# Attention values in one run per set, and a new order of ScalarE and VectorE work in the second pass of a sparse-attention and feed-forward kernel

## The chip, the cores and the metric

One core of a Trainium2 chip. The metric is the device time in microseconds of one execution, as the median of several runs; lower is better. A profile of one execution gives the times of single instructions.

## The reference

Block-sparse attention over 4 batches, 8 heads, 768 positions and a head size of 64, followed by a feed-forward layer with softplus between its two matrices. A position's block of 32 sees the neighbouring blocks, the first, the last, and three sampled ones; the rows of the first and last block see everything.

```python
def _attn_ref(q, k, v, sampled_blocks):
    scores = scale * np.matmul(q, k.transpose(0, 1, 3, 2))
    mask = np.abs(blk_i - blk_j) <= window
    mask = mask | (blk_i == 0) | (blk_j == 0) | (blk_i == n_blocks - 1) | (blk_j == n_blocks - 1)
    ...
            mask[qb * block:(qb + 1) * block, kb * block:(kb + 1) * block] = True
    scores = np.where(mask, scores, -1000000000.0)
    ...
    return np.matmul(attn, v)

def _moe_ref(x, w_in, w_out):          # x is 3072 x 512, d_ff 2048
    h = x @ w_in
    g = np.maximum(h, 0.0) + np.log1p(np.exp(-np.abs(h)))
    return g @ w_out
```

## The kernel before

**Attention.** The work is cut into 28 sets: per batch five sparse sets of four query blocks, a whole set (the first and last block, which see all keys) and a sparse set of the last two query blocks, folded onto the partitions. Each set has two units (`NA` is 2), a unit being four heads. A unit goes through `scores` (TensorE, PE below; then VectorE, DVE below, masks them, L831), `exponents` (ScalarE, ACT below, L881), `transposes` (PE L894, copied to SBUF tiles `pt`, of which there are four) and `values` (PE L937, L924 or L951: weights of 32 or 64 columns, so that several outputs lie side by side on the array). Both units of a set write one PSUM tile, which `normalise` reads after the second; `turn` transposes the result (L980) and `x_high` and `x_low` (L995, L999) split it into two parts for matmuls in two terms. The values of a set are partly gathered by indirect DMAs, which GpSimd (POOL below) issues (L764), into one of two buffers; `load_values` for the set after next is queued when a set's second unit has its values.

`pieces(n)` cuts a unit's work into three pieces, each with parts of several units: `scores` of unit n+2, then `exponents` of n+2, `turn` of the set before and `values` of n, then `transposes` of n+1.

**Feed-forward.** Its steps `j` run through `seq`: the first pass takes 6 of the 16 slices of d_ff for 8 tiles of 384 tokens (48 steps) and shares its time with attention, piece by piece by due times (`due`); the second pass takes the other 10 slices for 6 tiles of 512 tokens (60 steps). A step spreads over the following ones: `hidden(j)` is the first matrix (L268 to L270) with Abs and Exp on ACT (L272, L277; in combined steps also the relu, L275); `rounding(j)` the copy plus one on ACT (L283) and two operations on DVE (L285, and L287 or L289); then `logarithm` (ACT L294), `softplus` (DVE L316 or L322), `high` (ACT L347 or L343, the part rounded for the matmul), `low` (DVE L359 or L354, the rest) and, three steps later, `project`, the second matrix.

Forty steps of the second pass (tiles 1 to 4) are combined: two slices by two halves of the tokens are multiplied with seven products in place of eight. `combine` (POOL L337) forms the sums of the inputs, `project_item` (L437 to L439) adds into seven PSUM sums in seven banks, so that `h` has one bank in these steps. After the last slice of a tile, `store_item` puts the sums together for each half: two copies on ACT (L455, L457), four additions on DVE that read PSUM (L456, L458 to L460), then six additions on POOL (L464) and two stores, which `add_later` issues four at a time behind the `combine` of the next steps.

**What sets the order.** The order on SP, which issues most DMAs, is that of the program throughout. In the second pass the order on ACT, DVE and POOL is that of the program too. In the first pass these engines, and PE always, are ordered by a planner that follows the program's order with its own costs for each instruction.

```python
def first_half(j):
    for stage, n in ((high, j - 2), (logarithm, j - 1), (hidden, j)):
def second_half(j):
    for stage, n in (
        (softplus, j - 1), (combine, j - 1), (add_later, j - 1), (low, j - 2), (rounding, j), (project, j - LEAD)
    ):
```

Of the kernel before, what the change touches and what calls it, by code (L numbers as in the profile page):

```python
# [15 lines left out]
ALU = mybir.AluOpType  # L16
# [11 lines left out]
EARLY = 6  # L28
# [29 lines left out]
def sparse_attention_ffn(  # L58
# [22 lines left out]
    nc = tc.nc  # L81
# [4 lines left out]
    NA = NP // 2  # L86
# [8 lines left out]
    NTB = NT // TB  # L95
# [254 lines left out]
    def low(n):  # L350
# [5 lines left out]
        if not combined(n):  # L356
# [2 lines left out]
            nc.vector.tensor_tensor(out=gl, in0=l, in1=G[n].bitcast(F32), op=ALU.subtract)  # L359
            G[n] = (G[n], gl)  # L360

    def first_half(j):
        for stage, n in ((high, j - 2), (logarithm, j - 1), (hidden, j)):
            if 0 <= n < len(seq):
                stage(n)

# [35 lines left out]
    acc = {}  # L402
# [7 lines left out]
    def sums_of(half, m):  # L410
        if m == 4:
            return acc[2][:, half * SUB : (half + 1) * SUB]
        bank, at = ((0, 0), (1, 0), (1, 1), (2, 0), None, (0, 1), (2, 1))[m]
        return acc[half][bank][:, at * SUB : (at + 1) * SUB]
# [25 lines left out]
        if last:  # L440
            store_item(2 * t + half)

    later_sums = []

    def store_item(u):
        half = u % 2
        na, nb = 2 * u, 2 * u + 1
        ya, yb = Y.pop(na), Y.pop(nb)
        m1, u2, u3, m5 = [
            gp.tile([P, SUB], F32, tag=tag, name=f"{tag}_{u}_{x}") for tag in ("e", "u") for x in range(2)  # L450
        ] if half == 0 else [
            gp.tile([P, SUB], F32, tag=tag, name=f"{tag}_{u}_{x}") for tag in ("gh", "gl") for x in range(2)
        ]
        left, right = slice(0, SUB), slice(SUB, DM)
        nc.scalar.copy(out=m1, in_=sums_of(half, 0))  # L455
        nc.vector.tensor_tensor(out=yb, in0=acc[half][1], in1=yb, op=ALU.add)  # L456
        nc.scalar.copy(out=m5, in_=sums_of(half, 4))  # L457
        nc.vector.tensor_tensor(out=u2, in0=sums_of(half, 5), in1=m1, op=ALU.add)  # L458
        nc.vector.tensor_tensor(out=ya[:, left], in0=ya[:, left], in1=sums_of(half, 3), op=ALU.subtract)
        nc.vector.tensor_tensor(out=u3, in0=sums_of(half, 6), in1=u2, op=ALU.add)  # L460
        for out_, more in (
            (u2, m5), (m5, u3), (yb[:, left], m1), (yb[:, right], u2), (ya[:, left], u3), (ya[:, right], m5),
        ):
            later_sums.append((lambda o=out_, x=more: nc.gpsimd.tensor_tensor(out=o, in0=o, in1=x, op=ALU.add)))  # L464
        later_sums.append((lambda: put(nb, yb)))
        later_sums.append((lambda: put(na, ya)))

    def add_later(n):
        for _ in range(4):
            if later_sums:  # L470
                later_sums.pop(0)()
# [27 lines left out]
    def put(n, y):  # L499
        b, g = order[n]  # L500
        lo = b * S + (4 * g + 1) * BLOCK
        rows = P if g < NG - 1 else P - BLOCK
        nc.sync.dma_start(out=out[lo : lo + rows], in_=y[0:rows])
        if rows < P:
            nc.sync.dma_start(out=out[b * S : b * S + BLOCK], in_=y[rows:P])
# [45 lines left out]
    for rows in (slice(0, NR * BLOCK), slice(NR * BLOCK, P)):  # L551
# [4 lines left out]
        out=vbuf[0][:, 0, 0, :], out_offset=None, in_=v,  # L556
# [69 lines left out]
    def load_kT(b, n, engine=nc.sync, parts=4):  # L626
        load_part(b, n * NB // parts, (n + 1) * NB // parts, engine)
# [30 lines left out]
    def gathered(work, m):  # L658
        while work and work[0][0] <= m:
            work.pop(0)[1]()  # L660
# [54 lines left out]
    sets = []  # L715
# [62 lines left out]
    units = [(m, a) for m in range(len(sets)) for a in range(NA)]  # L778
# [127 lines left out]
    def values(n):  # L906
        m, a = units[n]
        b, g, whole = sets[m]
        pt = state[n]["pt"]
        gathered(value_work, m)  # L910
        vd = vg[sets[m]]
        if a == 0:
            xps[m] = ps_x.tile([P, DM], F32, tag="x", name=f"x{n}")
        xq = xps[m]

        if not whole and g == NG - 1:
            for r in range(2):
                at = (2 * a + r) * D
                for c in range(2):
                    for j in range(2):  # L920
                        h = 2 * (2 * a + j) + r
                        for i in range(2):
                            rows = slice((2 * j + i) * BLOCK, (2 * j + i + 1) * BLOCK)
                            nc.tensor.matmul(  # L924
                                xq[rows, at : at + D],
                                pt[r, c][:, rows],
                                vd[:, c, i, h * D : (h + 1) * D],
                                start=(c == 0), stop=(c == 1),
                            )
        elif not whole:  # L930
            for j in range(2):
                for r in range(2):
                    h = 2 * (2 * a + j) + r
                    for c in range(2):
                        for i in range(NI):
                            rows = slice(i * BLOCK, (i + 1) * BLOCK)
                            nc.tensor.matmul(  # L937
                                xq[rows, h * D : (h + 1) * D],
                                pt[r, 2 * j + c][:, rows],
                                vd[:, c, i, h * D : (h + 1) * D],  # L940
                                start=(c == 0), stop=(c == 1),
                            )
        else:
            rows_v = vd.rearrange("p c i f -> p (c i) f")
            for r in range(2):
                at = (2 * a + r) * D
                for c in range(NCH):
                    for o in range(2):
                        rows = slice(64 * o, 64 * o + 64)
                        h = 2 * (2 * a + o) + r  # L950
                        nc.tensor.matmul(  # L951
                            xq[rows, at : at + D],
                            pt[r, c][:, rows],
                            rows_v[:, c, h * D : (h + 1) * D],
                            start=(c == 0), stop=(c == NCH - 1),
                        )
# [47 lines left out]
    def pieces(n):  # L1004

        ended = [units[i][0] if 0 <= i < len(units) and units[i][1] == NA - 1 else None for i in range(n - 2, n + 1)]

        scored = None
        if n + 2 < len(units) and units[n + 2][1] == NA - 1 and not sets[units[n + 2][0]][2]:
            scored = place[sets[units[n + 2][0]][:2]]  # L1010

        def score_piece():
            if ended[0] is not None:
                x_low(ended[0])
            s = n + 2
            if s < len(units):
                scores(s)
                if scored is not None:
                    load_keys(scored + 2)
                m, a = units[s]  # L1020
                b, g, whole = sets[m]
                if whole and a == NA - 1 and b + 1 < B:

                    gathered(key_work, place[b, g])
                    for n_ in range(4):
                        load_kT(b + 1, n_)
                    load_keys()

        def value_piece():
            if n + 2 < len(units):  # L1030
                exponents(n + 2)
            if ended[1] is not None:
                turn(ended[1])
            if n < len(units):
                values(n)
                if ended[2] is not None:
                    load_values(ended[2] + 2)
            if scored is not None:
                load_queries(scored + 2)

        def transpose_piece():
            if ended[1] is not None:
                x_high(ended[1])
            if ended[2] is not None:
                normalise(ended[2])
            if n + 1 < len(units):
                transposes(n + 1)

        return score_piece, value_piece, transpose_piece


# [52 lines left out]
        gather()  # L1104
        convert()

    SECOND = NTB * EARLY
    owed = 0.0

    def convert():  # L1110
# [38 lines left out]
    for j in range(len(seq) + LEAD):  # L1149
        if j >= SECOND:  # L1150
            phase, t, f = seq[j] if j < len(seq) else (3, 0, 0)
# [4 lines left out]
        for i in range(NPAIR):  # L1156
            at = SECOND + LEAD + 1 + i
            if j == at:
# [3 lines left out]
            if j == at + 3 + (i == NPAIR - 1):  # L1162
                split_pair(i)
        if j == SECOND - 3:
            load_x(0)
        if j == SECOND:
            ctx.enter_context(tc.manual_schedule(
# [13 lines left out]
        if done == len(attention) and ahead is None:  # L1181
# [5 lines left out]
            ahead = EARLY  # L1187
        while ahead is not None and ahead < min(NF, EARLY + 2 * (j + EARLY - SECOND + 1)):
            load_w2(ahead)
            ahead += 1  # L1190

        for _ in range(1 + j % 2):
            if j >= SECOND - 4 and parked:
                split_w2(*parked.pop(0))
# [38 lines left out]
```

## Time and profile before

| | |
|---|---|
| median of 3 runs | 805.89 us (804.74 to 806.54) |
| the profiled execution | 804.17 us, span 802.4 us |
| PE busy | 764.1 us (95%) |
| DVE, ACT, POOL busy | 591.3, 562.0, 398.1 us |
| DMA | 132.27 MB, mean 165 GB/s |

Times are microseconds from the start of the span. PE is the matmul part of TensorE, PEld its weight loads. In a row of a group of instructions stand line, engine, operation, `out<-in` with the program's tile names, shape and count, then busy time, mean ns of one, and the idle time ahead of them with what ended it. A row of waits names who waited, for whom, the total, the number and the longest. In a timeline a row has start, duration, engine, line and, in brackets, the idle time before it. Up to about 65 us only attention runs; until about 420 us attention and the first pass share the core, and the second pass starts at about 461 us.

### The profile page before, as it was taken

The page shows a single profiled execution, that of the slowest core. Times are in us where ns is not written, and L with a number is a line of the kernel's source. Part 1 is how long each engine was busy: PE and PEld are TensorE (multiplying, and loading weights), DVE is VectorE, ACT ScalarE, POOL GpSimd, SP SyncE. Part 2 cuts the span into 40 slices and gives each one's busy share as a digit, 9 for nine tenths or more (in the row PEclk, how much of TensorE's full clock was granted, in tenths as well). Part 3 has the DMA queues.
Part 4 walks back from the last instruction along what each step waited for, and adds up shares of the span by engine and source line. Part 5 has one row for each costly group of instructions (what it writes and reads, how often), then busy time and mean ns, then how long its engine had stood idle before and what let it go on. Part 6 is the DMA issues. An engine that isn't in the chain of part 4 may idle for free.

```text
span 802.4 us, 21570 instructions
## 1 busy us (share of the span) xinstructions
PE 764.1 (95%) x8188; PEld 620.0 (77%) x8188; DVE 591.3 (74%) x1292; ACT 562.0 (70%) x1235; POOL 398.1 (50%) x617
## 2 busy tenths in 40 slices
PE   8779979999999999999999999999999999999997
PEld 7546657777778777687788888888988988988786
DVE  6678898787877777785664658886687787876654
ACT  4777878876877777776766766777666757756552
POOL 6783776544565427564000006435487686595400
PEclk9899989999999999999999999999999999999999
DMA  8878897678797686956525764330303215020021
GB/s 246 251 226 278 258 255 246 186 254 285 205 282 222 217 287 190 287 146 191 181 76 188 231 232 168 105 107 1 105 27 107 79 40 171 14 67 26 27 79 52
DMA packets 61174, 132.27 MB, mean 165 GB/s; under 512 B 5712, under 2 KB 18128, under 8 KB 60048
## 3 DMA queue, kind: packets, MB, share of 16 engines
q1 hardware_dynamic: 55072, 112.41, 44.4%
q0 software_dynamic: 5712, 17.57, 7.7%
q8 instruction: 64, 1.05, 0.6%
q10 hardware_dynamic: 288, 0.93, 0.3%
q14 instruction: 38, 0.31, 0.1%
HBM read 100.47 MB, written 30.41 MB: 163 GB/s over the span
## 4 chain that ended last, share of the span: by engine, by line
PE 49%; DVE 18%; ACT 17%; POOL 6%; issue 5%; DMA 3%; another core or an unknown queue 1%; SPq 0%; ACTq 0%; DVEq 0%; POOLq 0%
PE h L268 7%; PE h L270 6%; PE h L269 6%; ACT pr L881 6%; POOL gq L337 4%; PE o L486 4%; PE o L487 4%; PE o L488 4%; DVE e L285 3%; PE t L894 3%; PE x L937 3%; PE s L825 2%; DVE gl L359 2%; PE acc L439 2%; PE acc L438 2%
## 5 line engine op out<-in xcount | busy, mean ns | idle before, releaser
L337 POOL TENSOR_TENSOR gq<-gq 128x128 f32<-128x128 f32 x160 | 112.1, 723 | 76.3 <-DVE gq L322 73.2
L285 DVE SCALAR_TENSOR_TENSOR e<-u,e 128x512 f32<-128x512 f32 (+1 forms) x108 | 84.5, 782 | 84.8 <-ACT u L283 81.7
L881 ACT ACTIVATE pr<-pr,nmax 128x256 f32<-128x256 f32 (+1 forms) x192 | 102.2, 534 | 30.9 <-DVE nmax L831 14.1
L764 POOL DMA_INDIRECT vg<-in_v_dram,ix x88 | 88.2, 1003 | 67.8 <-PE x L937 38.6
L706 POOL COPY kg<-kT 128x128 f32 x252 | 88.2, 394 | 44.5 <-PE s L825 38.3
L272 ACT ACTIVATE e<-h 128x512 f32<-128x512 f32 (+1 forms) x108 | 58.8, 544 | 71.5 <-PE h L270 71.2
L268 PE MATMUL h<-x,w 128*128 128x512 f32 x240 | 95.8, 399 | 6.4 <-ACT gh L275 4.9
L270 PE MATMUL h<-x,w 128*128 128x512 f32 x240 | 94.6, 394 | 0.0
L269 PE MATMUL h<-x,w 128*128 128x512 f32 x240 | 94.6, 394 | 0.0
L294 ACT ACTIVATE u<-u 128x512 f32<-128x512 f32 (+1 forms) x108 | 62.9, 582 | 24.2 <-DVE e L285 23.5
L193 POOL TENSOR_TENSOR wt<-wt,raw 128x512 int32<-128x512 int32 x32 | 43.5, 1360 | 68.8 <-ACT raw L170 51.8
L283 ACT ACTIVATE u<-e 128x512 f32<-128x512 f32 (+1 forms) x108 | 63.1, 584 | 17.9 <-DVE gl L359 14.3
L268 PE MATMUL h<-x,w1all 128*128 128x384 f32 x192 | 69.0, 360 | 3.4 <-DVE e L289 2.3
L831 DVE CUSTOM_DVE_ANT_1 pr<-s,mask 128x256 f32<-128x256 f32 x160 | 58.2, 418 | 16.8 <-PE s L825 8.8
L894 PE MATMUL t<-ident,pr 128*128 128x128 f32 x448 | 65.2, 286 | 4.4 <-DVE nmax L831 2.0
L343 ACT CAST w1all<-gq 128x896 fp32r<-128x896 f32 x40 | 37.7, 942 | 39.4 <-POOL gq L337 37.4
L270 PE MATMUL h<-x,w1all 128*128 128x384 f32 x192 | 65.2, 340 | 0.0
L269 PE MATMUL h<-x,w1all 128*128 128x384 f32 x192 | 65.2, 340 | 0.0
L277 ACT ACTIVATE e<-e 128x512 f32<-128x512 f32 (+1 forms) x108 | 63.1, 584 | 1.8
L486 PE MATMUL o<-w1all,gh 128*128 128x512 f32 x144 | 61.0, 424 | 0.0
L894 PEld LDWEIGHTS t<-ident,pr 128*128 128x128 f32 x448 | 50.8, 145 | 13.0 <-issue 2.7
L268 PEld LDWEIGHTS h<-x,w 128*128 128x128 f32 x240 | 45.0, 188 | 17.9 <-ACT gh L275 6.3
(141 smaller groups left out, 2051.1 us busy)
## 6 DMA issues: line engine op xcount, KB each, us to landing
vg<-in_v_dram SPq DMA_DIRECT2D x19, 768.0 KB
xD<-x SPq DMA_DIRECT2D x8, 1536.0 KB
raw<-in_w_in_dram SPq DMA_DIRECT2D x16, 512.0 KB
raw<-in_w_out_dram SPq DMA_DIRECT2D x16, 512.0 KB
qc<-in_q_dram SPq DMA_DIRECT2D x24, 256.0 KB
vg<-in_v_dram SPq DMA_DIRECT2D x12, 512.0 KB
yD<-os SPq DMA_DIRECT2D x24, 256.0 KB
x<-xD SPq DMA_DIRECT2D x4, 1536.0 KB
```

Source lines behind the costliest of these rows:

```text
L268: nc.tensor.matmul(ph, wh[:, cols], hi[:, c], start=(c == 0), stop=False)
L269: nc.tensor.matmul(ph, wh[:, cols], lo[:, c], start=False, stop=False)
L270: nc.tensor.matmul(ph, wl[:, cols], hi[:, c], start=False, stop=(c == NC - 1))
L277: nc.scalar.activation(e, e, AF.Exp, scale=-1.0)
L283: nc.scalar.activation(u, e, AF.Copy, bias=1.0)
L285: nc.vector.scalar_tensor_tensor(out=e, in0=u, scalar=-1.0, in1=e, op0=ALU.add, op1=ALU.subtract)
L337: nc.gpsimd.tensor_tensor(out=a[:, to], in0=a[:, x], in1=a[:, y], op=op)
L486: nc.tensor.matmul(po[m], gh[:, cols], wh, start=first, stop=False)
L706: copy(out=kd[:, i, 1 + NR + s, :], in_=kT[b][:, bass.ds(x, 1), :].rearrange("p n f -> p (n f)"))
L764: nc.gpsimd.indirect_dma_start(out=vd[0 : 3 * BLOCK, 1, i, :], out_offset=None, in_=v, in_offset=bass.IndirectOffsetOnAxis(ap=ix[:, b, 4 * ...
L881: nc.scalar.activation(x, x, AF.Exp, bias=nmax[rows, r, j : j + 1], scale=-1.0, accum_out=rs[rows, h : h + 1])
L894: nc.tensor.transpose(ps[:, i, 0:rows], st["pr"][r][0:rows, c * P : (c + 1) * P], ident[0:rows, 0:rows])
```

## The change

Three edits. In `pieces`, the values of a sparse set are no longer issued unit by unit: those of the first unit wait, and both units' values are issued in the place of the second. Whole sets keep theirs; `load_values` stays where it was. In `first_half`, from the second pass on, the logarithm of step j-1 stands ahead of the high part of step j-2. In `store_item`, the four DVE additions are kept back; `add_later` issues them in the next step, behind its softplus and combine, and ahead of the POOL additions that need them.

```diff
+    SECOND = NTB * EARLY
+
     def first_half(j):
-        for stage, n in ((high, j - 2), (logarithm, j - 1), (hidden, j)):
+        steps = ((high, j - 2), (logarithm, j - 1)) if j < SECOND else ((logarithm, j - 1), (high, j - 2))
+        for stage, n in (*steps, (hidden, j)):
             if 0 <= n < len(seq):
                 stage(n)
...
-    later_sums = []
+    later_sums, next_sums = [], []
...
         nc.scalar.copy(out=m1, in_=sums_of(half, 0))
-        nc.vector.tensor_tensor(out=yb, in0=acc[half][1], in1=yb, op=ALU.add)
         nc.scalar.copy(out=m5, in_=sums_of(half, 4))
-        nc.vector.tensor_tensor(out=u2, in0=sums_of(half, 5), in1=m1, op=ALU.add)
-        nc.vector.tensor_tensor(out=ya[:, left], in0=ya[:, left], in1=sums_of(half, 3), op=ALU.subtract)
-        nc.vector.tensor_tensor(out=u3, in0=sums_of(half, 6), in1=u2, op=ALU.add)
+
+        def rest():
+            nc.vector.tensor_tensor(out=yb, in0=acc[half][1], in1=yb, op=ALU.add)
+            nc.vector.tensor_tensor(out=u2, in0=sums_of(half, 5), in1=m1, op=ALU.add)
+            nc.vector.tensor_tensor(out=ya[:, left], in0=ya[:, left], in1=sums_of(half, 3), op=ALU.subtract)
+            nc.vector.tensor_tensor(out=u3, in0=sums_of(half, 6), in1=u2, op=ALU.add)
+
+        next_sums.append(rest)
...
     def add_later(n):
+        if next_sums:
+            next_sums.pop()()
         for _ in range(4):
...
             if n < len(units):
-                values(n)
-                if ended[2] is not None:
-                    load_values(ended[2] + 2)
+                m, a = units[n]
+                if sets[m][2]:
+                    values(n)
+                elif a == NA - 1:
+                    for n_ in range(n - NA + 1, n + 1):
+                        values(n_)
+                if a == NA - 1:
+                    load_values(m + 2)
```

More of the change, by code (lines that the diff above doesn't have):

```diff
@@ L1105, in attend @@
         convert()
-    SECOND = NTB * EARLY
     owed = 0.0
```

## The prediction

> **What bounds the kernel now.** I read the page's engine totals first, then busy time by stage, then the idle time ahead of the matmuls and the chain of waits at one place where they stopped.
>
> ```profile
> span 802.4 us, 21570 instructions
> PE 764.1 (95%) x8188; PEld 620.0 (77%) x8188; DVE 591.3 (74%) x1292; ACT 562.0 (70%) x1235; POOL 398.1 (50%) x617
> 0.00:65.00 65.00, 52.28 (x944) 38.82 (x944) 42.76 (x156) 43.13 (x113) 45.90 (x95) 0.92 0.84 249
> 125.00:420.00 295.00, 287.07 (x4393) 222.60 (x4386) 222.22 (x614) 220.78 (x570) 137.72 (x239) 1.00 0.71 215
> 540.00:730.00 190.00, 185.08 (x1154) 165.29 (x1153) 146.28 (x200) 130.80 (x223) 134.00 (x179) 1.00 0.21 69
> ```
>
> TensorE sets the pace: busy 287.1 of 295 us where attention and the first pass share it, and 185.1 of 190 us in the combined steps of the second pass. The columns after the stretch are PE, PEld, DVE, ACT, POOL, the granted clock, the DMA share and GB/s. What is left to win in those two stretches is 7.9 and 4.9 us of idle time, plus whatever makes PE's work shorter. DVE and ACT, at 222 and 221 of 295 us, have a quarter of their time free, but only on average.
>
> In the second pass nearly all of PE's idle time has one name (us in total, times, longest):
>
> ```profile
> PE h L268 <- ACT gh L275: 4.9, 7, 1.2
> ```
>
> The first matmul of a step waits for L275, the relu that empties the only PSUM bank left for `h`: 4.9 us on PE, seven times. One such place, as the chain of waits has it (start, time, what):
>
> ```profile
> 589.99 0.66 DVE y L456
> 590.65 0.33 DVE gh L458
> 591.23 0.41 DVE gl L460
> 591.64 0.34 DVE gq L322
> 592.05 2.72 POOL gq L337 x3
> ...
> 607.08 0.47 POOL gq L337
> 607.58 0.94 ACT w1all L343
> 608.52 0.53 ACT u L294
> 609.05 0.48 ACT e L272
> 609.53 0.49 ACT gh L275
> 610.07 0.50 PE h L268
> 610.57 0.23 PE h L269
> ```
>
> Read upwards from 610.07: PE waits for relu, relu for Abs, Abs stands behind the logarithm (L294) and the cast of `high` (L343), the cast waits for GpSimd's combine (L337), and GpSimd has been in unbroken work since 592.05, when it had to wait for the softplus (L322), which stood behind the additions of `store_item` (L456 to L460).
>
> **The change, part by part.**
>
> **Additions behind the next softplus.** No instruction is added or removed; four DVE additions move past two halves of L322. From 589.99 to 591.64 they take 1.65 us, so the softplus could run, and the combine start, up to 1.65 us earlier, at 590.4. GpSimd itself must be free then:
>
> ```profile
> 585.13 0.79 POOL L464 TENSOR_TENSOR e<-e,u 128x256 f32<-128x256 f32 x1 [0.87 <-DVE u L460]
> 586.75 2.75 POOL L464 TENSOR_TENSOR y<-y,e 128x256 f32<-128x256 f32 x2
> 592.05 3.59 POOL L337 TENSOR_TENSOR gq<-gq 128x128 f32<-128x128 f32 x4 [2.55 <-DVE gq L322]
> ```
>
> It idles 2.55 us before 592.05, because its additions ended at 589.50. Those additions read what the moved ones write, and for the first half they now start behind a softplus as well, at about 586 instead of 585.13; they then end near 590.4. So the combine gains 1.6 us at each of the three inner boundaries. The other waiters: the two stores of a row leave SP's queue by as much later as the sum is late, with loads behind them that are due a whole row later, at no cost; the PSUM sums are read before the next row's first `project_item` opens them, since that is one step later; at the last boundary the plain `o` tiles take over those banks after one softplus more, at most 0.7 us once (as long as L456), which I leave at 0 because PE has a `hidden` to run before it.
>
> **Logarithm ahead of the high part.** One exchange on ACT in each step of the second pass. At 607.58 the logarithm no longer stands between the cast and Abs: 0.53 us off the chain. The price: the logarithm waits for DVE's L285, which then delays the cast.
>
> ```profile
> ACT e L272 <- PE h L270: 6.9, 6, 1.4
> ACT u L294 <- DVE e L285: 0.5, 1, 0.5
> ```
>
> In the stretch 560 to 620 us ACT waits up to 1.4 us for the next `h` in an undisturbed step, and the logarithm waited for L285 once, 0.5 us. The exchange moves the wait and costs nothing while that slack is there; without it, it would cost up to 0.5 us a step. `low` of the cast tile follows `high` on DVE later by one logarithm, in time that DVE spends waiting for L283.
>
> The sum for the second pass: the idle time is 4.9 us, and each of the seven restarts shows a first matmul of 0.50 against 0.23 us, 7 x 0.27 = 1.9 us more, so 6.8 us at most. Over the three inner boundaries that is some 2.2 us each; the two relieved pieces, 1.6 and 0.53, make 2.1, just about enough. I allow 0.3 us left over in each of the three and 0.2 where the combined steps begin: -6.8 + 1.1 = -5.7 us. Ends: -6.8, and +2 if POOL's chain stays as long and the logarithm's wait of 0.5 us is paid at four boundaries.
>
> A sentence on a rule against it. The Trainium skill, PSUM — Partial Sum Buffer, section "Engine vs sequencer instructions", says that the queues of ScalarE, VectorE and GpSimdE are strictly first in, first out; by that, a logarithm that waits 0.5 us holds cast and Abs as well, and four boundaries would give back 2 us of the 5.7. The trace agrees that ACT ran nothing else in that wait.
>
> **Values of both units in one run.** The same 64 records a unit, moved from the first unit's place to the second's, past one step's scores, hidden and projection. What changes on PE is the number of entries into and exits from the 128*32 tiles:
>
> ```profile
> 240.72 0.60 PE L980 MATMUL y<-ident,xs 128*128 128x128 f32 x4
> 241.24 1.10 PE L937 MATMUL x<-vg,pt 128*32 128x64 f32 x64
> 242.28 1.28 PE L894 MATMUL t<-ident,pr 128*128 128x128 f32 x8
> 243.31 0.44 PE L268 MATMUL h<-x,w1all 128*128 128x384 f32 x1
> 248.92 1.10 PE L937 MATMUL x<-vg,pt 128*32 128x64 f32 x64
> 249.95 1.09 PE L894 MATMUL t<-ident,pr 128*128 128x128 f32 x8
> 250.80 0.42 PE L268 MATMUL h<-x,w1all 128*128 128x384 f32 x1
> L937 PE MATMUL x<-vg,pt 128*32 128x64 f32 x1856 | 33.9, 221 | 1.9 <-issue 1.9
> L924 PE MATMUL x<-vg,pt 128*32 128x64 f32 x128 | 2.9, 223 | 0.0
> ```
>
> A run lasts 1.10 us with a last matmul of 0.22, so the pitch is 0.88/63 = 14 ns; but the next kind starts 1.03 us after the first, so the exit costs 0.15 - 0.014 = 0.136 us. On entry, four transposes of 0.28 in 0.60 us have a pitch of 0.107, and the fourth is followed by the values after 0.52 - 0.32 = 0.20: 0.09 more. One exit and one entry less make 0.23 us a set. Between 125 and 420 us lie 1856/128 = 14.5 sparse sets and two folded ones: 16 x 0.23 = 3.7 us.
>
> Against it stands the cover. In the first unit's step PE has 1.12 us less to do, in the second's 0.89 more. What bounds a step besides PE is the round from `hidden` over ACT and DVE back to a free bank:
>
> ```profile
> 241.31 0.42 DVE L831 CUSTOM_DVE_ANT_1 pr<-s,mask 128x256 f32<-128x256 f32 x1 [1.46 <-PE y L980]
> 242.69 0.56 DVE L289 SCALAR_TENSOR_TENSOR e<-h,e 128x384 f32<-128x384 f32 x1
> DVE pr L831 <- PE y L980: 5.9, 4, 2.2
> ```
>
> L289, which frees the bank of `h`, ended at 243.25 and the next `hidden` began at 243.31: here the 1.03 us of values were cover, and PE would idle instead. In such a set the net is +0.9, in one with slack -0.23. The long step before it lets ACT and DVE catch up, so I take the middle of what both leave, about 0 for the 16 sets (ends -3.7 and +14). The later values also need two more `pt` tiles at once, and four are there.
>
> Then there are stops inside runs that nothing in the profile explains:
>
> ```profile
> 362.41 0.91 POOL L764 DMA_INDIRECT vg<-in_v_dram,ix  x1 [0.30 <-issue]
> 363.63 0.91 POOL L764 DMA_INDIRECT vg<-in_v_dram,ix  x1 [0.30 <-issue]
> 363.54 0.42 PE L937 MATMUL x<-vg,pt 128*32 128x64 f32 x14
> 365.64 0.96 PE L937 MATMUL x<-vg,pt 128*32 128x64 f32 x46 [1.10 <-issue]
> PE x L937 <- issue: 5.6, 12, 1.1
> ```
>
> They fall in first units' runs, next to GpSimd's indirect loads, which `load_values` queues after each second unit. In the new place the runs stand away from them. Of 5.6 us (1.9 after 125 us, the rest before 65 us, where gathers and DMA at a share of 0.84 also bound the time) I count 1.9: ends 0 and -5.6. The DMA issues of the moved step stay where they were on SP and POOL. The Trainium skill, Runtime: NRT & Kernel Launch, section "Instruction fetch mechanics", says that instruction blocks are prefetched in sequence and the fetch is hidden; by that, these stops are not starved fetches and a run twice as long adds none, and the sum stays. No row here names their cause.
>
> The sum: 804.17 (the profiled execution) - 5.7 + 0 - 1.9 = 796.6. The median of the runs shown is 805.89, 1.7 higher; on that scale it is 798.3, and I forecast 798.
>
> **The rivals.**
> Cover lost, which ends on the other side: in the first unit's step PE waits for the bank of `h`, as at 243.31, and the second's grows by 0.89. All 16 sets: +14.2 - 5.7 = +8.5, 814. It decides above 5.7/16 = 0.36 us a set. For it: L289's 0.06 us of margin at 243.31. Against it: at 250.80 `hidden` started while L289 of the step before had not ended, and DVE has a quarter of its time free.
> All of the first pass comes true: -5.7 - 3.7 - 5.6 = -15.0, 791. For it: the exits are regular to 10 ns. Against it: the early stops lie in a stretch that PE does not bound alone.
> GpSimd stays the bound at the boundaries, or the waiting logarithm holds Abs: of 5.7 us 3.6 are lost, 802: then only the logarithm's 0.53 us is won in four places, 2.1 us. For it: POOL works without a pause from 592.05 to 607.55, and its additions start later than now. Against it: the 2.55 us that it idles before.
> The edits cancel: the first pass loses what the second wins, 806.
>
> **How the numbers follow.** Forecast 0.42, all of the first pass 0.25, boundaries only in part 0.12, cancelled 0.08, cover lost 0.13. Faster by over 0.2% (about what a measurement here tells from no change, 1.6 us) is 0.42 + 0.25 + 0.12 = 0.79, no difference 0.08, slower 0.13. The range must take in 791 with some of what is above -15 and half of the cover's loss: 789 to 808. The forecast's own range is 795 to 802.
>
> **What would show it.** Second pass: L268's wait for L275 falls from 4.9 us to under 1.2; L322 stands ahead of L456 on DVE; POOL's pause before L337 shortens by 1.6 us; the combined steps keep their pace across boundaries. First pass: runs of L937 with 128 records that last about 2 us, half as many exits, the step that now runs from 243.31 to 250.80 grows to 8.4 us and the one ahead of it shrinks by up to 1.1; "issue" ahead of L937 under 2 us. I am wrong if L268 in the first pass waits for L289 or L999 in every second step, if L294's wait for L285 in the second pass exceeds 1 us a step, or if the planner, which orders PE in both passes, breaks the runs up.

## The result, and the profile after

The changed kernel is slower: 813.96 us median (810.77 to 818.1) against 807.06 us (804.74 to 810.41) for the kernel before, ratio 1.009, 95% interval 1.0071 to 1.0109. Forecast was 798 us in a range of 789 to 808. The profiled execution took 815.21 us, 11.0 more than the profiled one before.

Line numbers move by nine behind `add_later` (`scores` L834, its mask L840, `transposes` L903, `values` L946, `turn` L989) and by five to seven at `store_item` (additions L462 to L465, POOL's L471). The span, the totals and busy time by stage (columns PE, PEld, DVE, ACT, POOL, clock, DMA share, GB/s), after:

```profile
span 813.4 us, 21594 instructions
PE 767.1 (94%) x8188; PEld 620.3 (76%) x8188; DVE 597.6 (73%) x1292; ACT 564.1 (69%) x1235; POOL 400.8 (49%) x617
0.00:65.00 65.00, 52.85 (x875) 38.23 (x879) 39.46 (x151) 38.95 (x101) 44.03 (x95) 0.87 0.78 225
125.00:420.00 295.00, 277.19 (x4309) 213.37 (x4310) 220.80 (x606) 215.53 (x558) 141.05 (x240) 0.99 0.72 223
540.00:730.00 190.00, 188.93 (x1161) 168.32 (x1160) 155.26 (x208) 136.56 (x230) 135.39 (x177) 1.00 0.22 71
```

The two stages went opposite ways. In the second pass PE's idle time fell from 4.9 to 1.1 of 190 us; from the first `hidden` of that pass to the end of the span are 337.0 us, 340.8 before. In the first pass the idle time rose from 7.9 to 17.8 of 295 us, and the second pass began at 476.4 instead of 461.6 us. Most of the rest of these 14.8 us lies before 125 us, where the granted clock was lower in this execution as well (0.87 against 0.92 up to 65 us, 0.89 against 0.94 from there). What PE waited for over the whole span, the first row from before and the others from after (us, times, longest):

```profile
PE t L894 <- DVE nmax L831: 2.0, 3, 1.1
...
PE t L903 <- DVE nmax L840: 10.2, 13, 1.9
PE s L834 <- DVE nmax L840: 4.2, 1, 4.2
PE s L834 <- ACT pt L910: 3.1, 5, 1.4
PE h L268 <- DVE e L289: 2.6, 3, 2.1
PE x L946 <- issue: 2.0, 1, 2.0
PE h L268 <- ACT gh L275: 1.1, 3, 0.4
```

The last row is the second pass, mended. The largest grew from 2.0 us in three places to 10.2 in thirteen: the transposes of the probabilities wait for the masks, 5.6 us of it between 125 and 420 us. The 4.2 us are one stop at 23.85 us; at that place `e14` and `e15` below, with the values moved and not moved, stop too (4.0 and 3.6 us), so it hardly comes from the change. One place of the first kind, PE first, then DVE:

```profile
172.44 1.09 PE L834 MATMUL s<-kg,qc 64*32 64x256 f32 x32
175.68 0.60 PE L989 MATMUL y<-ident,xs 128*128 128x128 f32 x4
177.86 1.32 PE L903 MATMUL t<-ident,pr 128*128 128x128 f32 x8 [1.59 <-PE y L989]
178.94 0.44 PE L268 MATMUL h<-x,w1all 128*128 128x384 f32 x1
...
174.18 0.56 DVE L285 SCALAR_TENSOR_TENSOR e<-u,e 128x384 f32<-128x384 f32 x1 [0.33 <-issue]
176.94 0.42 DVE L840 CUSTOM_DVE_ANT_1 pr<-s,mask 128x256 f32<-128x256 f32 x1 [2.20 <-PE y L989]
178.32 0.55 DVE L289 SCALAR_TENSOR_TENSOR e<-h,e 128x384 f32<-128x384 f32 x1
```

This is a first unit's step, where the values used to stand between `turn` and the transposes. The four banks that `scores`, `turn`, transposes and `hidden` share are full: the first four transposes take the bank of one `s`, the next four that of the other, and the next `h` the one that L289 frees. So PE stops at 176.27 until the first two masks are done at 177.71, 1.59 us until it starts again. (The profile puts this wait, and that of the mask at 176.94, down to the turn, `PE y`, whose release came last; the transposes need the banks, and DVE ran nothing between 174.74 and 176.94.)

### The profile page after: what moved, and what is told of

Same layout as the page of the kernel before. It is cut to its first block, busy times and chain, and to the rows that moved or that the text cites. A ratio compares the mean times of both kernels' runs of the same rounds, so it can differ in the third digit from the quotient of the medians.

```text
span 813.4 us, 21594 instructions
## 1 busy us (share of the span) xinstructions
PE 767.1 (94%) x8188; PEld 620.3 (76%) x8188; DVE 597.6 (73%) x1292; ACT 564.1 (69%) x1235; POOL 400.8 (49%) x617
## 4 chain that ended last, share of the span: by engine, by line
PE 62%; ACT 13%; DVE 12%; POOL 7%; issue 3%; DMA 1%; another core or an unknown queue 1%; SPq 0%; DVEq 0%; POOLq 0%; ACTq 0%
PE h L268 9%; PE h L270 8%; PE h L269 8%; PE o L495 5%; PE o L496 5%; PE o L497 5%; PE s L834 4%; PE t L903 4%; ACT pr L890 4%; PE x L946 4%; POOL gq L337 3%; DVE e L285 3%; POOL y L471 2%; PE acc L442 2%; PE acc L441 2%
## 5 line engine op out<-in xcount | busy, mean ns | idle before, releaser
L285 DVE SCALAR_TENSOR_TENSOR e<-u,e 128x512 f32<-128x512 f32 (+1 forms) x108 | 89.2, 826 | 96.7 <-ACT u L283 90.5
L773 POOL DMA_INDIRECT vg<-in_v_dram,ix x88 | 86.5, 983 | 68.5 <-PE x L946 39.4
L715 POOL COPY kg<-kT 128x128 f32 x252 | 89.6, 399 | 55.8 <-PE s L834 52.7
L294 ACT ACTIVATE u<-u 128x512 f32<-128x512 f32 (+1 forms) x108 | 63.0, 584 | 74.2 <-DVE e L285 70.7
L903 PE MATMUL t<-ident,pr 128*128 128x128 f32 x448 | 66.3, 285 | 17.1 <-DVE nmax L840 10.2
L193 POOL TENSOR_TENSOR wt<-wt,raw 128x512 int32<-128x512 int32 x32 | 43.2, 1349 | 72.8 <-ACT raw L170 38.6
L840 DVE CUSTOM_DVE_ANT_1 pr<-s,mask 128x256 f32<-128x256 f32 x160 | 58.5, 418 | 24.9 <-PE s L834 10.1
L268 PE MATMUL h<-x,w1all 128*128 128x384 f32 x192 | 70.1, 365 | 3.2 <-DVE e L289 2.1
L903 PEld LDWEIGHTS t<-ident,pr 128*128 128x128 f32 x448 | 50.5, 145 | 29.0 <-issue 7.8
L834 PE MATMUL s<-kg,qc 64*32 64x256 f32 x1280 | 58.6, 405 | 9.4 <-DVE nmax L840 4.2
L270 PE MATMUL h<-x,w1all 128*128 128x384 f32 x192 | 66.2, 345 | 0.5 <-issue 0.5
L269 PE MATMUL h<-x,w1all 128*128 128x384 f32 x192 | 66.0, 344 | 0.0
L495 PE MATMUL o<-w1all,gh 128*128 128x512 f32 x144 | 60.7, 422 | 0.0
L496 PE MATMUL o<-w1all,gh 128*128 128x512 f32 x144 | 57.4, 399 | 0.0
```

Source lines behind the costliest of these rows:

```text
L268: nc.tensor.matmul(ph, wh[:, cols], hi[:, c], start=(c == 0), stop=False)
L269: nc.tensor.matmul(ph, wh[:, cols], lo[:, c], start=False, stop=False)
L270: nc.tensor.matmul(ph, wl[:, cols], hi[:, c], start=False, stop=(c == NC - 1))
L285: nc.vector.scalar_tensor_tensor(out=e, in0=u, scalar=-1.0, in1=e, op0=ALU.add, op1=ALU.subtract)
L495: nc.tensor.matmul(po[m], gh[:, cols], wh, start=first, stop=False)
L496: nc.tensor.matmul(po[m], gh[:, cols], wl, start=False, stop=False)
```

## The two halves of the change apart

Each ratio is to the kernel before in the same comparison: that took 795 us in two of the later comparisons and 807 to 808 us in three, as in the first.

**Second pass alone** (`e1`, repeated as `e10`, `e15`, `e19`): the values at their old place (code shortened).

```
-                if sets[m][2]: values(n)
-                elif a == NA - 1: (both units)
+                values(n)
```

> Only the two edits of the second pass (logarithm ahead of the high part, additions behind the next softplus); the values stay where they were. Theory (the values lose some 11 us in the first part, the second pass wins 3.8): the first matmul of the second pass starts at 461 to 462 us as before, and the time is 3.5 to 4.5 us under before, ratio 0.995. Rival (the loss in the first part comes from elsewhere, for instance from another order that the planner finds once the program is changed at all): the second pass starts late here too, by more than 3 us, and the time is not under before.

> The two edits of the second pass alone once more, beside the others on one chip: 0.997 of before as in the first comparison (interval 0.995 to 0.999).

792.82 us against 795.3, ratio 0.997 (0.9952 to 0.9989); repeated 0.9975 (0.9955 to 0.9994), 0.9967 (0.9947 to 0.9987) and 0.9954 (0.9927 to 0.9982), that is 2.2 to 3.9 us. In the profile 337.8 us remain from the second pass on, 3.0 less than before. The 2.5 us between the medians are less than the 3.5 to 4.5 expected of `e1`, and the 0.997 expected of the repeats held.

**Values alone** (`e2`): the two other edits undone.

> Only the values of both units in one run; the second pass as before. Theory: the whole loss is here, the second pass starts 14 to 15 us later than before, and the time is 10 to 14 us over before (ratio 1.013 to 1.017). Rival: values and second-pass edits hurt each other only together; then this kernel is within 4 us of before.

799.73 us against 795.3, ratio 1.0055 (1.0036 to 1.0075): 4.4 us lost, so the loss is here, though less than half of what I expected from the two first traces. From the start of the second pass it takes 340.8 us, as before. Two of PE's waits ahead of the second pass that differ most, for `e1` and then for `e2`:

```profile
PE t L903 <- DVE x L1008: 4.8, 2, 3.2
PE t L903 <- DVE nmax L840: 2.3, 4, 1.1
...
PE x L945 <- issue: 6.3, 4, 3.2
PE t L902 <- DVE nmax L839: 5.9, 6, 2.7
```

Waits for masks grow by 3.6 us, and stops appear inside the merged runs, for which `e1` has no row; the wait for the cast of the turned set (L1008) becomes smaller.

**Logarithm alone** (`e3`) and **additions alone** (`e4`):

```
e3:  next_sums.append(rest)  ->  rest()
e4:  steps = ((logarithm, j - 1), (high, j - 2))  ->  ((high, j - 2), (logarithm, j - 1))
```

> Only the logarithm ahead of the high part. If the 0.53 us of the logarithm at each boundary are worth what they last, four places give -2.1 us; if the combine on GpSimd sets the boundary, it gives nothing (within 1 us), as the cast waits for GpSimd whatever stands before it; if the logarithm's wait for the rounding of DVE is on the path, it costs up to +2 us.

> Only the additions from PSUM behind the next softplus. If GpSimd's chain sets the three inner boundaries, its earlier start is worth 1.6 us at each as far as the wait at the boundary reaches: -2.5 to -3.5 us. If the logarithm before Abs sets it, nothing (within 1 us).

Logarithm: 1.001 (0.999 to 1.003), nothing, as the second of its three expectations has it. Additions: 0.998 (0.9964 to 0.9996), 1.7 us, less than the 2.5 to 3.5 expected. The three steps around the first inner boundary, from one first `hidden` matmul to the next in each trace, show how they combine (undisturbed 3 x 5.24 = 15.72 us):

| kernel | steps | sum |
|---|---|---|
| before | 5.89, 5.34, 6.56 | 17.79 |
| logarithm (e3) | 5.66, 5.35, 6.95 | 17.96 |
| additions (e4) | 5.24, 5.24, 6.57 | 17.05 |
| both (after) | 5.31, 5.30, 5.80 | 16.41 |

Alone, the logarithm's exchange buys nothing, since the cast still waits for GpSimd (2.58 us ahead of the cast at 600.73 in `e3`); with the additions moved it buys 0.64 us at this boundary, about the 0.53 that it lasts.

## The cover: tests of the first pass

**The changed kernel again** (`e7`), and beside the second-pass edits (`e14` beside `e15`), gives the whole loss within one comparison.

> The changed kernel once more, to stand beside the others of this group on one chip. If the parts simply add (second pass -0.3%, values +0.55%), its ratio to before is 1.0025; if it is as in the first comparison, 1.009. In the trace: scores whose completion reaches VectorE late by 1 to 3 us after the matmul's record, as at 173.5 us of the first one, if the loss depends on them; else none.

> The changed kernel beside the second-pass edits alone. If the parts add: 1.0025 of before where the kernel before takes 795 us, 1.007 to 1.009 where it takes 807; in both cases 4 us or more over e15.

> The second-pass edits alone, as the base of e12 and e13: 0.997 of before, whatever before takes.

`e7` 1.007 (1.0045 to 1.0095), `e14` 1.0069 (1.0044 to 1.0094): not the 1.0025 of added parts. The kernel before against itself, beside `e7` (`e8`), gives 0.9989 (0.9965 to 1.0014). The late masks that `e7` was to show are there: scores end at 171.0 us and their masks start 3.4 us later, with DVE idle for 2.2. `e14` is 812.51 us, `e15` 804.41: the values' move costs 8.1 us where the kernel before takes 807 us, and 4.4 (`e2`) where it takes 795. The stretch from 125 to 420 us and PE's waits in it, `e15` and then `e14`:

```profile
125.00:420.00 295.00, 285.38 (x4391) 220.34 (x4373) 222.94 (x607) 218.50 (x563) 134.17 (x239) 0.99 0.70 214
PE t L903 <- DVE nmax L840: 0.4, 1, 0.4
PE s L834 <- ACT pt L910: 0.8, 2, 0.6
...
125.00:420.00 295.00, 277.55 (x4366) 213.27 (x4358) 220.87 (x602) 216.76 (x559) 140.45 (x240) 1.00 0.73 221
PE t L903 <- DVE nmax L840: 5.5, 9, 1.6
PE s L834 <- ACT pt L910: 3.1, 5, 1.3
```

PE's idle time grows from 9.6 to 17.5 us, by 7.8: transposes that wait for masks grow by 5.1 and scores that wait for the copies of the transposes by 2.3; smaller rows go both ways.

**The same work twice** (`e5`): the first unit's values at both places (code shortened).

```
 elif a == 0:
     values(n)          # and again below
 else:
     for n_ in range(n - NA + 1, n + 1): values(n_)
```

> The changed kernel, with the first unit's values also computed in their old place (the same records a second time, 64 a set more, some 1.03 us a set, about 16 us of TensorE work in all; the result is the same). Cover lost: the work fills waits that are there now, so the time is not more than 8 us over the changed kernel, and the wait of the transposes for the masks (10 us in the changed kernel's first trace) falls under 3 us. Rival, TensorE has no room in those steps and the loss comes from elsewhere (the start, DMA, the longer second step): 15 to 17 us over the changed kernel.

815.78 us, ratio 1.0097 (1.0059 to 1.0135), beside 813.73 for `e7`: 2.1 us more. The totals and the wait, `e7` and then `e5`:

```profile
PE 764.0 (94%) x8188; PEld 617.7 (76%) x8188; DVE 598.0 (74%) x1292; ACT 564.0 (69%) x1235; POOL 400.5 (49%) x617
PE t L903 <- DVE nmax L840: 10.9, 12, 2.4
...
PE 781.9 (96%) x9596; PEld 640.0 (78%) x9596; DVE 596.1 (73%) x1292; ACT 565.8 (69%) x1235; POOL 401.5 (49%) x617
PE t L903 <- DVE nmax L840: 1.7, 2, 1.3
```

1408 matmuls more, 17.9 us more of busy time, and 2.1 us of time between the medians, 5.0 between the two profiled executions: most of the work fell into time in which PE had stood still, and the wait for the masks is nearly gone, as the first of the two theories has it. (1408 = 20 x 64 + 4 x 32, so 24 sets are merged; the expectation spoke of the 16 between 125 and 420 us.)

**The turn behind the transposes** (`e6`, repeated as `e11`; code in short): the spare bank then goes to the first four transposes.

```
 value_piece:      -  turn(ended[1])
 transpose_piece:  -  x_high(ended[1])    # ahead of normalise and transposes
                   +  turn(ended[1]); x_high(ended[1])    # behind transposes(n + 1)
```

> The changed kernel with the turn (transposes of the finished set, and the cast behind them) moved behind the transposes of the probabilities, so that the first transposes of a first unit's step take the spare bank and only the second four wait for a mask. If the bank that the masks hold is what the step waits for: 3 to 8 us under the changed kernel. Rival, the mask itself is late and everything behind it waits whatever stands first: within 2 us of the changed kernel, or over it, as the transposes then begin 0.43 us earlier and wait longer.

> The changed kernel with the late turn once more, beside e9 and e10 on one chip. If one run of values for both units is worth its saved switch (0.23 to 0.27 us a set, 3.7 us in all) once the first unit's step no longer waits: 2 to 4 us under e9. If the cover is still partly missing, it is level with e9 or over it by up to 4 us.

806.42 us beside 813.73 for `e7`, ratio 0.9976 (0.9943 to 1.0008): 7.3 us won back by an exchange that removes no instruction, in the 3 to 8 that the theory of the bank gives. The bank is what the step waits for. In the 795 us comparison `e11` has 793.14 us, 0.9966 (0.9949 to 0.9983). Waits remain, and stand where this order puts them, at the second four transposes (the first row, which the profile puts down to the first four) and at the turn, `e6`:

```profile
PE t L903 <- PE t L903: 4.4, 3, 1.8
PE t L903 <- DVE nmax L840: 2.2, 5, 0.6
PE y L989 <- DVE nmax L840: 4.7, 2, 4.0
```

**Late turn without the merged values** (`e9`).

> Both edits of the second pass, the values in their old places, and the turn behind the transposes of the probabilities. It tells what the late turn is worth when the cover is there. If the late turn helps only by freeing the spare bank in a step without values: within 2 us of e10 (the same without the late turn). If TensorE waited for banks in the old order too (some 3 to 5 us of waits of transposes for masks and for x_low in the trace of before): 2 to 5 us under e10.

794.37 us, 0.998 (0.9962 to 0.9997), beside 793.43 for `e10`: where the cover is there, the late turn is worth nothing. And `e11` is 1.2 us under `e9`, less than the 2 to 4 of saved switches, and each ratio lies in the other's interval: the saved switches are not shown as time.

**Half of the values left out**, in the first unit's step (`e12`) or in the second's (`e13`), old order (code shortened; these kernels leave out the second of a unit's two chunks):

```
- for c in range(2):
+ for c in range(2 if a == 1 else 1):      # e12; a == 0 in e13
```

> The second-pass edits, values in their old places, but the first unit of each sparse set multiplies only the first of its two chunks (32 records of 64 left out, some 0.45 us a set, 7 us of TensorE work in all). If the first unit's values are cover for the masks: 0 to 3 us under e15. If TensorE has no other wait there: 6 to 8 us under it.

> The same with the second unit's values halved instead. If TensorE is the bound of the second unit's step, where no turn comes and the masks have been read: 5 to 8 us under e15, and 3 us or more under e12. If the two steps are alike, e12 and e13 are within 2 us.

793.96 and 793.31 us, ratios 0.9826 (0.9794 to 0.9857) and 0.9812 (0.9774 to 0.9851): 10.4 and 11.1 us under `e15`. Both expectations of `e12` missed: the first unit's values weren't free in the old order. Of `e13`'s, that the two steps are alike held (0.65 us apart). 640 records fewer at 14 ns are 9.0 us, so both are paid in full. `e12`, a first unit's step, and its waits over the whole span:

```profile
163.32 0.60 PE L989 MATMUL y<-ident,xs 128*128 128x128 f32 x4
163.84 0.65 PE L946 MATMUL x<-vg,pt 128*32 128x64 f32 x32
164.43 1.09 PE L903 MATMUL t<-ident,pr 128*128 128x128 f32 x8
165.28 0.42 PE L268 MATMUL h<-x,w1all 128*128 128x384 f32 x1
...
PE t L903 <- DVE nmax L840: 4.7, 7, 1.6
```

With half of the values the transposes mostly start without a wait; it grows to 4.7 us in seven places, from 1.6 in three (`e15`), and between 125 and 420 us it is 1.2 us. So the cover that is needed seems to lie between nothing and about half of the 1.03 us, a threshold and not a share; no run took all of the first unit's values out with the second's left as they were, which would show it. Why these two save a little more than the records' time isn't settled.

## What is left at the boundaries of the second pass

GpSimd still works without a pause up to the cast at an inner boundary. The chain in the changed kernel, and at its end PE's restart:

```profile
605.45 1.45 POOL gq L337 x3
...
607.44 2.70 POOL y L471 x2
...
615.78 1.76 POOL y L471 x2
...
620.62 0.54 POOL gq L337
621.18 0.94 ACT w1all L343
622.13 0.49 ACT e L272
622.62 0.50 ACT gh L275
623.16 0.50 PE h L268
```

The logarithm is out of it; cast, Abs and relu follow each other. `e16` spreads POOL's additions three a step, `e19` is its base, `e18` puts it on `e6`.

```
-        for _ in range(4):                      # additions and stores
+        room = 3                                # additions; stores go along
```

> The two second-pass edits, and GpSimd's additions behind a finished row spread three a step over four steps instead of four, two, four, two (stores as before). If GpSimd's chain still sets the inner boundaries: one addition of 0.88 us less ahead of the last combine ends the waits of 0.27 to 0.39 us there, 0.5 to 0.7 us a boundary, 1.5 to 2 us in all under e19. If the rest is ScalarE's cast, Abs and relu in a row: within 0.3 us in the trace of the second pass.

> The two second-pass edits alone, as the base of e16: 0.997 of before.

> The same on the changed kernel with the late turn. If the gains are independent: under e11's ratio of 0.9966 by 0.002, and level with e16 or up to 2 us under it. Rival: where the kernel before takes 807 us, the merged run still waits for masks, and it is 2 us or more over e16.

`e16` 0.9968 (0.9945 to 0.9991), `e19` 0.9954 (0.9927 to 0.9982), `e18` 0.9995 (0.9969 to 1.0021). No gain: in `e16` the same three waits of PE for L275 stand one step later (618.35, 671.76 and 725.13 us, 0.35 to 0.41 us each, against 0.27 to 0.38 in `e19`), as GpSimd's work is the same in total; the second pass takes 338.6 us in its trace and 337.7 in `e19`'s. One addition less ahead of that combine only moved the wait, so both theories of the leftover fell; that less work on GpSimd would end it was not tried. `e18` is 3.3 us over `e19` by the medians, with intervals that overlap, and 1.8 over `e16`: the gains don't add, and its rival's 2 us or more was just missed.

The version to keep is the second-pass edits alone: under before in all four comparisons.

## Why the prediction was wrong

**The cover, priced at 0, is the step that failed.** I took the middle between -3.7 and +14 us because "the long step before it lets ACT and DVE catch up". Measured, as the whole of the move: +4.4 and +8.1 us. The rival "cover lost" had the sign, and 814 us for a time of 814, but not its place: PE waits at the transposes for the banks of the scores, not at `hidden` for L289. The row that I quoted (L289's margin of 0.06 us) looked at the bank of `h` alone. The masks stood in the same fence, L831 at 241.31, behind an idle DVE, 2.74 us after the scores ended; I did not ask which PE instruction takes the bank that they free. The amount of that rival came out right by luck: it priced 0.89 us a set in all 16, and the waits for masks between 125 and 420 us are 5.6 us in nine places.

**The switch, -3.7 us, was right in its own rows** and doesn't show in the time. Where the masks come early, a pair of steps is shorter by what I worked out. `e2`, the starts of three `hidden` and the run between:

```profile
158.49 0.42 PE L268 MATMUL h<-x,w1all 128*128 128x384 f32 x1
163.99 0.60 PE L988 MATMUL y<-ident,xs 128*128 128x128 f32 x4
164.43 1.04 PE L902 MATMUL t<-ident,pr 128*128 128x128 f32 x8
165.22 0.42 PE L268 MATMUL h<-x,w1all 128*128 128x384 f32 x1
170.82 1.99 PE L945 MATMUL x<-vg,pt 128*32 128x64 f32 x128
173.60 0.42 PE L268 MATMUL h<-x,w1all 128*128 128x384 f32 x1
162.98 0.42 DVE L839 CUSTOM_DVE_ANT_1 pr<-s,mask 128x256 f32<-128x256 f32 x1
```

6.73 and 8.38 us, 15.11 the pair, against 15.38 (7.90 and 7.48) before: 0.27 won, 0.23 forecast. The last row is the mask of the same step: here it starts 1.1 us after the scores end (161.85), in the changed kernel's trace 3.4 us after (173.53 and 176.94), and there the step takes 8.77. One wait of 1.6 us eats six saved switches.

**Second pass, -5.7 us:** the mechanism was right, the size too large by 1.9 us or more: 3.8 us in the first two traces, 2.2 to 3.9 between medians. I put 2.2 us at an inner boundary and left 0.3; there were 2.07 (17.79 against 15.72), and 0.69 stayed, so the three boundaries gave 4.1. POOL's pause there is 2.36 us and was 3.42 (0.87 and 2.55): 1.06 shorter, not 1.6, as its own additions now wait for the four moved ones:

```profile
600.82 1.45 POOL L471 TENSOR_TENSOR e<-e,u 128x256 f32<-128x256 f32 x1 [2.36 <-DVE u L465]
```

At the last boundary, which I left at 0, the five steps from 729.97 us before and 740.25 after take 0.37 us more. L294's wait for L285 rose from 1.9 us in 5 steps to 48.3 in 51, near the 1 us a step at which I would be wrong, and did no visible harm: undisturbed steps keep their 5.24 us, and Abs still waits 34.1 us for `h` in the second pass. The rule of the Trainium skill that I set against the sum (PSUM — Partial Sum Buffer, "Engine vs sequencer instructions") fits that row, as ACT stands still in it, and costs nothing that these steps show.

**Stops, -1.9 us:** in the runs of values they fell from 5.6 us in 12 places to 2.0 in one, but not where I counted them: after 125 us there were 1.9 us in four places, and there the 2.0 stand in one (355.25 us). So this term gave nothing. `e5`, with a run at the old place, stops there again (at 175.68, 1.12 us). In the first 795 us comparison it went the other way, from no row to 6.3 us in four places. So that a run twice as long adds no stops, which I took along with a rule on instruction blocks (the Trainium skill, Runtime: NRT & Kernel Launch, "Instruction fetch mechanics"), isn't borne out; whether fetches cause them, no run here shows.

## What to carry to other kernels

Before work is moved away from between two instructions of the busiest engine, ask of each bank that the later one takes who frees it and when; the work in between may be the only time that this has. Here half of a cover was mostly enough, and without it one set could lose 1.6 us, six times what the move saves it. Where two edits shorten one chain, try them together as well: in the steps of the boundary the logarithm alone gave nothing, the additions alone 0.74 us, and both 1.38.

## What the runs showed of the hardware

Completion of matmuls can reach another engine well after the record's end: scores that end at 173.53 by their record started the masks at 176.94, with DVE idle for 2.20 us; in `e2` the two times are 161.85 and 162.98. The unchanged kernel has it too: in the trace of before the masks at 241.31 start 2.74 us after their scores, with DVE idle for 1.46, and in `e1` those of the same place (231.15) 1.19 us after, with DVE not idle. Between 125 and 420 us, masks that start over 1.5 us after their scores behind a DVE idle for over 1 us stand in two to six places in each of the 13 traces from comparisons at 807 us, before included, and in none of the seven at 795. So the larger price of the move (8.1 against 4.4 us) goes with late masks that the values covered in the old order; that they alone make the difference isn't shown. The Trainium skill, Perfetto Trace Analysis, section "Tensor Engine Instruction (MATMUL, LD_WEIGHTS)", says that a matmul's reported end is an estimate from its size and that the semaphore is pushed only when PSUM has acknowledged the write; the trace agrees that such a record's end isn't the release. What delays it by microseconds in some comparisons and not in others stays open. So does the cause of the stops in the runs of values: in the kernels with all values in their old places they come to 5.2 to 9.6 us in the traces at 807 us and to at most 0.7 at 795, but with the values moved there are 6.3 us at 795 (`e2`) and 2.0 to 2.6 at 807.

DVE's shift of the weights took five times as long beside GpSimd's addition L193, in the changed kernel:

```profile
139.90 2.03 DVE L183 TENSOR_SCALAR wt<-wt 128x512 int32<-128x512 int32 x1
140.32 1.31 POOL L193 TENSOR_TENSOR wt<-wt,raw 128x512 int32<-128x512 int32 x1
169.45 0.41 DVE L183 TENSOR_SCALAR wt<-wt 128x512 int32<-128x512 int32 x1
```

The Trainium skill, SBUF — State Buffer, section "SBUF: two separate sides", says that DVE, in its two-port modes or with two inputs in SBUF, and GpSimd share a pair of ports that one of them holds for a whole instruction; the first two rows agree, since L183 ends 0.30 us after L193. Beside GpSimd's copies (L715) the same instruction took 0.41 to 0.54 us in this trace, so not every instruction of GpSimd holds it up, and whether L183 runs in such a mode no run shows. The masks of that step (143.11 us) stand behind it, and PE waits 1.59 us ahead of 144.03: a static order of DVE's work, too, can take the cover away.
